# Spectral product by one inverse matmul: real and imaginary rows exchanged by DMA

## The chip, the cores and the metric

The kernel runs on one core of a Trainium2 chip. The metric is device time in microseconds, the median of several runs; one further execution was profiled. The engines are named as in the profile: PE (TensorE matmul; PEld is its weight load), DVE (VectorE), ACT (ScalarE), POOL (GpSimd) and SP (SyncE, which issues most DMAs).

## The reference, cut to what matters

Two layers follow each other. The first is an attention without softmax; the second is a long convolution by FFT between two gates. B is 8, S is 3136, D is 256, and z has 64 columns.

```python
scores = z @ z.T / S
x = u * (np.maximum(scores, 0) ** 2 @ v)          # 8 x 3136 x 256

x1, x2, x3 = split(x @ w_proj, 3)                 # 3136 x 256 each
X2 = rfft(x2, axis=1); H = rfft(filter_fft, axis=0)
y = x1 * irfft(X2 * H, axis=1) * x3
out = y @ w_out
```

`X2 * H` is a product of complex numbers, for each frequency and column. It is what the change is about.

## The kernel before, in words

**Attention.** A batch has 25 tiles of 128 rows (`NT`) and is worked through in seven chunks of 384 to 512 columns (`CHUNKS`). For each pair of tiles PE makes scores (L1238), ACT applies relu into `R_t` (L1388), DVE or ACT squares into `A_t` (L1397, L1395), and PE weighs the rows of v with the squares (L1266). The scores are symmetric, so squares of up to two chunks ahead are not computed again: SP issues DMA transposes of `A_t` into mirror tiles (`M_t`, `M2e_t`, `M2o_t`, L1351). An `A_t` buffer (there are 8) is free when its weighing and its transposes are done.

**Projection.** DVE multiplies the sum by u into `xT_t` (L1437). Then PE makes x1 and x3 (L821, L833), whose product goes to a tile of the ring `gate` (L839; 22 tiles, two a chunk), and x2 (L867).

**Convolution.** The transform of length 3136 is done as 64 x 49. A first stage (L699) works on x2 and stores its result to a scratch in DRAM (L706). When a batch is complete, `add_spectrum` runs over its 32 values of q in eight groups of four. For each group, SP loads four slices (L729) and PE makes the forward transform with the table `S2` (L912), one matmul of 98x256 for each q. The 98 rows of the result are 49 frequencies with a real and an imaginary row each, side by side. Two evictions (`copy`, L337 on ACT or L341 on DVE) bring them to `xs_t`. Then DVE multiplies the group by the filter's real and imaginary parts into the two halves of `zs_t`, in one instruction of 98x2048 (L934). The filter table `H` holds both parts with each repeated on both rows of a frequency. PE makes the inverse transform with two matmuls for each q (L956): the table `TZ[0]` for the half with the real part, and `TZ[1]`, whose rows are exchanged and signed, for the half with the imaginary part. They add up in PSUM, so the exchange of real and imaginary rows that a complex product needs is done by the second table. Evictions to `gs_t` and a store (L979) follow. The inverse matmuls of a group are handed to the planner after the forward part of the next group.

**End.** `add_end` loads the result (L740), makes the last transform stage (L1010), multiplies by the gates into `yT_t` (L1017), multiplies by w_out (L1048), evicts to `ost_t` and stores (L1075).

**Order of the work.** A planner in the kernel's own Python writes the order of every engine's instructions. Each piece of work is a task with a cost, its dependencies, the buffers that it takes, and a priority. PE's tasks lie in queues: S for scores, W for weighing, FA for projection, FB for the spectrum and the end, FZ for what is held back to the last batch. Side work is mixed into W by a credit (`PACE` 0.6 us for each W task). The other engines take the task that can start first, and at equal times the lower priority number. A DMA's landing is planned as the end of its issue, plus `DMA_GO` of 1.2, plus its `moves` on one shared bus, plus `DMA_DONE` of 0.8, plus a `late` of its own. All engines then run their lists in order. The last batch (7) has nothing behind it; there the spectrum and the end use buffers of the attention as well, and the rest of batch 6's end fills the gaps.

**Start.** The tables are made on the chip in the first 160 us, while batch 0 already runs: `S2` by sines, `TZ` by transposes on PE (L641; L671 for the reversed one, out of tiles that DVE makes, L665 and L666), `H` by a transform of the filter (L781) with tables from L768.

Of the kernel before, what the change touches and what calls it, by code (L numbers as in the profile page):

```python
# [11 lines left out]
P = 128  # L12
# [7 lines left out]
N2 = 49  # L20
NQ = 32
# [4 lines left out]
LATE_PUT, LATE_LOAD, LATE_TURN, LATE_C, LATE_D2 = 3.0, 1.0, 1.5, 2.5, 1.0  # L26
REACH = 2
# [211 lines left out]
def kernel(  # L239
# [59 lines left out]
    g_p = Pool("gate", 22, [P, 512], BF16)  # L299
# [3 lines left out]
    xs_p = Pool("xs", 2, [P, 4, D], BF16)  # L303
    zs_p = Pool("zs", 2, [P, 4, 2, D], BF16)
# [210 lines left out]
    TZ = const.tile([P, 2, NQ, KR], BF16, name="TZ")  # L515
    H = const.tile([P, NQ, 2, D], BF16, name="H")
# [117 lines left out]
    for q0 in range(0, NQ, 8):  # L634
        deps = [s2_done[q0], s2_done[q0 + 4]]
        box = {}

        def turn(q0=q0, box=box):
            box["p"] = bank(BF16)
            for i in range(8):  # L640
                nc.tensor.transpose(box["p"][:KR, ds(i * KR, KR)], S2[:KR, q0 + i, :], ident[:KR, :KR])  # L641

        def back(e, q0=q0, box=box):
            src = box["p"][:KR, 0 : 8 * KR].rearrange("p (q k) -> p q k", q=8)
            copy(e, TZ[:KR, 0, ds(q0, 8), :], src)

        tt = pe("FB", turn, c_pe(*[P] * 8), deps, takes=[ps_m.slots])
        tb = job(None, back, {"DVE": c_dve2(8 * KR)}, [tt], prio=3)
        tb.frees.append((tt, 0))
        tz_done.append(tb)  # L650
        if q0 == 0:
            tz_done.append(
                on(
                    "DVE",
                    lambda: nc.vector.tensor_single_scalar(TZ[0:2, 0, 0, :], TZ[0:2, 0, 0, :], 0.5, ALU.mult),
                    0.25, [tb],
                )
            )
        jbox = {}

        def sj(q0=q0, jbox=jbox):
            t = l_p.tile([P, 8, N2, 2], BF16)
            jbox["s"] = t
            sv = S2[:KR, ds(q0, 8), :].rearrange("p q (k c) -> p q k c", c=2)
            nc.vector.tensor_copy(t[:KR, :, :, 0], sv[:, :, :, 1])  # L665
            nc.vector.tensor_single_scalar(t[:KR, :, :, 1], sv[:, :, :, 0], -1.0, ALU.mult)  # L666

        def turnj(jbox=jbox):
            jbox["p"] = bank(BF16)
            for i in range(8):  # L670
                nc.tensor.transpose(  # L671
                    jbox["p"][:KR, ds(i * KR, KR)], jbox["s"][:KR, i, :, :].rearrange("p k c -> p (k c)"),
                    ident[:KR, :KR],
                )

        def backj(e, q0=q0, jbox=jbox):
            src = jbox["p"][:KR, 0 : 8 * KR].rearrange("p (q k) -> p q k", q=8)
            copy(e, TZ[:KR, 1, ds(q0, 8), :], src)

        ts = on("DVE", sj, 0.8, deps, [l_p.slots], prio=3)  # L680
        tt = pe("FB", turnj, c_pe(*[P] * 8), [ts], takes=[ps_m.slots])
        tt.frees.append((ts, 0))
        tb = job(None, backj, {"DVE": c_dve2(8 * KR)}, [tt], prio=3)
        tb.frees.append((tt, 0))
        tz_done.append(tb)
# [72 lines left out]
    for qq in range(NQ // 4):  # L758
# [3 lines left out]
        def tabs(qq=qq, tbox=tbox):  # L762
            t = gs_p.tile([P, 4, 2, KR], BF16)
            tbox["t"] = t
            for i in range(2):
                o = t[:KR, :, i, :].rearrange("p q (k c) -> p q k c", c=2)
                s = S2[:KR, ds(qq * 4, 4), :].rearrange("p q (k c) -> p q k c", c=2)
                nc.vector.tensor_copy(o, s[:, :, :, i].unsqueeze(3).to_broadcast([KR, 4, N2, 2]))  # L768
            if qq == 0:
                nc.vector.tensor_copy(t[:KR, 0, 0, 1:2], S2[:KR, 0, 1:2])  # L770
                nc.vector.memset(t[:KR, 0, 1, 0:2], 0.0)

        tb = on("DVE", tabs, 0.8, [s2_done[qq * 4], ld], [gs_p.slots], prio=3)
        for i in range(4):
# [11 lines left out]
            def ev(e, q=q, box=box):  # L786
                copy(e, H[:KR, q, :, :].rearrange("p i d -> p (i d)"), box["p"][:KR, :], h_scale)

# [103 lines left out]
    def add_spectrum(b, puts):  # L892
        deps0 = list(h_done) + list(tz_done) if b == 0 else []
        lasts = []
        prev = None
        for qq in range(8):
            own = b < B - 1 or qq % 2 == 0
            xh, zh, gh = (xs_p, zs_p, gs_p) if own else (xT_p, R_p, A_p)
            ld, ibox = load_spec(D1[b % 2], qq, puts, LATE_LOAD * (b < B - 1))
# [3 lines left out]
            for h in range(2):  # L903
                box = {}

                def mm(qq=qq, h=h, box=box, xb=xb, ibox=ibox, xh=xh, zh=zh):
                    box["p"] = bank()
                    if h == 0:
                        xb["x"], xb["z"] = xh.tile([P, 4, D], BF16), zh.tile([P, 4, 2, D], BF16)
                    for i in range(2):  # L910
                        q = qq * 4 + h * 2 + i
                        nc.tensor.matmul(  # L912
                            box["p"][:KR, ds(i * D, D)], S2[:KR, q, :], ibox["t"][:KR, h * 2 + i, :],
                            start=True, stop=True,
                        )

                def ev(e, h=h, box=box, xb=xb):
                    copy(e, xb["x"][:KR, ds(h * 2, 2), :].rearrange("p q d -> p (q d)"), box["p"][:KR, :])

                a = pe(  # L920
                    "FB", mm, c_pe(D, D), [ld, *deps0, *firsts],
                    [ps_m.slots] + ([xh.slots, zh.slots] if h == 0 else []),
                )
# [8 lines left out]

            def mul(qq=qq, xb=xb):
                nc.vector.tensor_tensor(  # L934
                    xb["z"][:KR], xb["x"][:KR].unsqueeze(2).to_broadcast([KR, 4, 2, D]),
                    H[:KR, ds(qq * 4, 4), :, :], ALU.mult,
                )

            z_ = on("DVE", mul, c_dve2(8 * D), evs)
            z_.frees.append((a0, 1))  # L940

            def inv(qq=qq, xb=xb, z_=z_, a0=a0, gh=gh):
# [3 lines left out]
                for h in range(2):  # L946
                    box = {}

                    def mm(h=h, box=box):
# [3 lines left out]
                        for i in range(2):  # L953
                            q = qq * 4 + h * 2 + i
                            for k in range(2):
                                nc.tensor.matmul(  # L956
                                    box["p"][:KR, ds(i * D, D)], TZ[:KR, k, q, :], xb["z"][:KR, h * 2 + i, k, :],
                                    start=(k == 0), stop=(k == 1),
                                )

                    def ev(e, h=h, box=box):
# [3 lines left out]
                        "FB", mm, c_pe(D, D, D, D), [z_, *firsts],  # L965
# [3 lines left out]
                    if h == 0:  # L969
                        g0 = a  # L970
                    else:
                        a.frees.append((a0, 2))
# [8 lines left out]
                p_ = on("SP", put, 0.4, es, moves=1.0, late=LATE_D2 * (b < B - 1))  # L981
# [3 lines left out]
            if prev:  # L985
                prev()
            prev = inv
        prev()
# [4 lines left out]
    def add_end(b, lasts, gtasks, tg, kind="FB", src=l_p, dsts=(o_p,), late=0, behind=(), then=()):  # L993
        for t0, nt in tg:
# [7 lines left out]
            for dh in range(2):  # L1002
# [26 lines left out]
                e_ = on("DVE", ev, 0.068 * pieces + w * 0.00104, [a], prio=2 + late)  # L1029
# [95 lines left out]
    def casts_at(b, c):  # L1125
# [3 lines left out]
        if n < B and 0 <= i < 4:  # L1129
            t0, t1 = 8 * i, min(8 * i + 8, NT)  # L1130

            def go_z(tick_):
# [27 lines left out]
                z_tasks.setdefault(n, []).append(t)  # L1160

# [199 lines left out]
    for gi, g in enumerate(groups):  # L1361
# [16 lines left out]
        for i, un in enumerate(g):  # L1378
# [40 lines left out]
            if last:  # L1419
# [27 lines left out]
                if c == NC - 1:  # L1447
# [9 lines left out]
                    else:  # L1457
                        add_end(b, lasts, gts, ends, "FB", A_p, (R_p, zs_p))
# [53 lines left out]
```

## Time and profile before

| what | value |
|---|---|
| runs | 1083.94 us median of 3 (1081.19 to 1084.87) |
| profiled execution | 1083.45 us, span 1081.7 us, mean granted clock 0.988 |
| PE | 1029.6 us busy, 6517 recorded matmuls |
| ACT, DVE, POOL | 910.7, 811.2, 184.8 us busy |
| DMA | 324112 packets, 167.44 MB, mean 155 GB/s |
| L956, inverse matmuls in PSUM tile `ps_m_t` | 456 recorded, mean 275 ns |
| L934, product with the filter, 98x2048 | 60, mean 1219 ns |
| L979, stores of the inverse transform | 60 of 196 KB |

The page of the profile gives for each engine its busy time, its share of the span and its instructions. The span is then cut into 40 slices, with a digit of tenths for each. The chain is followed back from the last instruction to what released each step. Groups of instructions stand by line, engine and tile. Matmuls are pipelined: a record lasts longer than the step from one matmul's start to the next. A small share of the matmul records is missing.

### The profile page before, as it was taken

The numbers are of one execution on the slowest core, as the hardware profiler recorded it, in microseconds if no ns is written. First come the engines' busy times: TensorE is split into PE (matmuls) and PEld (weight loads), VectorE is DVE, ScalarE is ACT, GpSimd is POOL, SyncE is SP. The second block draws the span as 40 slices with busy tenths as digits, with TensorE's granted clock in tenths as the row PEclk, the third lists the DMA queues.
The fourth block names the chain that finished last, engine by engine and source line by source line (L and its number), as shares of the span: only waits on it lengthen the run. The fifth ranks groups of instructions, "written<-read, shape, count | busy, mean of one in ns | idle before, by whom it ended". The sixth has DMA issues, their size and how long they took to land.

```text
span 1081.7 us, 18827 instructions
## 1 busy us (share of the span) xinstructions
PE 1029.6 (95%) x6517; PEld 545.9 (50%) x6591; DVE 811.2 (75%) x1277; ACT 910.7 (84%) x1265; POOL 184.8 (17%) x351
## 2 busy tenths in 40 slices
PE   5999899999999999999999999999999999999974
PEld 2444545545455455555455554555555554555563
DVE  7976679778777686977877687876878668776673
ACT  6987799888888888987889898898979879798763
POOL 2022202121112210122021211121112220011000
PEclk9999999999999999999999999999999999999987
DMA  7488938886798978898688878898788996755556
GB/s 150 94 143 161 178 74 165 155 165 153 168 151 141 175 143 154 177 156 182 136 185 154 162 148 174 163 151 170 161 164 146 137 182 132 186 115 124 131 171 215
DMA packets 324112, 167.44 MB, mean 155 GB/s; under 512 B 231968, under 2 KB 293792, under 8 KB 324016
## 3 DMA queue, kind: packets, MB, share of 16 engines
q1 hardware_dynamic: 301552, 135.58, 57.1%
q0 software_dynamic: 22464, 30.65, 20.4%
q8 instruction: 52, 0.85, 0.3%
q14 instruction: 44, 0.36, 0.1%
HBM read 89.62 MB, written 53.05 MB: 132 GB/s over the span
## 4 chain that ended last, share of the span: by engine, by line
PE 84%; DVE 6%; DMA 5%; issue 2%; ACT 2%; POOL 0%; SPq 0%; DVEq 0%; ACTq 0%; POOLq 0%
PE ps_o_t L1266 44%; PE ps_s_t L1238 11%; PE ps_m_t L956 4%; PE ps_m_t L833 4%; PE ps_m_t L821 4%; PE ps_m_t L867 4%; PE ps_m_t L1048 4%; DMA M_t<-A_t 3%; PE ps_m_t L912 2%; PE ps_m_t L699 2%; DVE A_t L1397 2%; PE ps_m_t L1010 2%; DVE xT_t L1437 1%; ACT A_t L1395 1%; PE ps_m_t L781 1%
## 5 line engine op out<-in xcount | busy, mean ns | idle before, releaser
L1388 ACT ACTIVATE R_t<-ps_s_t 128x1024 f32<-128x1024 f32 (+3 forms) x552 | 484.2, 913 | 45.0 <-PE ps_s_t L1238 28.7
L1266 PE MATMUL ps_o_t<-A_t,v_t 128*128 128x512 bf16 (+2 forms) x2121 | 489.8, 355 | 5.6 <-issue 1.7
L1266 PEld LDWEIGHTS <-v_t 128*128 128x128 bf16 x2800 | 264.7, 98 | 210.7 <-issue 33.1
L1397 DVE TENSOR_TENSOR A_t<-R_t 128x1024 bf16<-128x1024 f32 (+3 forms) x298 | 320.8, 1085 | 53.9 <-ACT R_t L1388 22.1
L1395 ACT ACTIVATE A_t<-R_t 128x768 bf16<-128x768 f32 (+3 forms) x254 | 237.1, 940 | 25.2 <-DMA M_t<-A_t 10.8
L375 POOL COPY tick<-xT_t 1x1 bf16<-1x1 bf16 x54 | 42.5, 786 | 788.8 <-DVE xT_t L1437 759.0
L1238 PE MATMUL ps_s_t<-zT_t 64*128 64x512 bf16 (+2 forms) x1088 | 155.2, 359 | 1.9 <-DVE zT_t L341 0.8
L1437 DVE SCALAR_TENSOR_TENSOR xT_t<-ps_o_t,uT_t 128x384 bf16<-128x384 f32 (+2 forms) x128 | 69.9, 556 | 48.2 <-PE ps_o_t L1266 31.2
L341 DVE CAST x_t<-ps_m_t 128x512 bf16<-128x512 f32 (+3 forms) x121 | 72.7, 613 | 26.9 <-PE ps_m_t L867 18.1
L839 DVE TENSOR_TENSOR gate_t<-ps_m_t,x_t 128x512 bf16<-128x512 f32 (+2 forms) x112 | 67.3, 620 | 27.3 <-PE ps_m_t L833 21.5
L1238 PEld LDWEIGHTS <-zT_t 64*128 64x128 bf16 x1088 | 32.8, 94 | 101.1 <-issue 97.8
L934 DVE TENSOR_TENSOR zs_t<-xs_t,H 98x2048 bf16<-98x2048 bf16 x60 | 73.0, 1219 | 10.4 <-ACT xs_t L337 9.8
L1266 PE MATMUL ps_o_t<-M_t,v_t 128*128 128x384 bf16 (+2 forms) x336 | 79.4, 345 | 0.0
L956 PE MATMUL ps_m_t<-zs_t,TZ 98*98 98x256 bf16 x456 | 68.7, 275 | 4.1 <-ACT xs_t L337 3.5
L1017 DVE TENSOR_TENSOR yT_t<-ps_m_t,gate_t 128x128 bf16<-128x128 f32 (+3 forms) x163 | 62.7, 425 | 12.1 <-PE ps_m_t L1010 11.9
L956 PEld LDWEIGHTS <-TZ 98*98 98x98 bf16 x512 | 59.0, 126 | 24.2 <-issue 13.5
L337 ACT ACTIVATE x_t<-ps_m_t 128x512 bf16<-128x512 f32 (+3 forms) x106 | 55.8, 540 | 15.5 <-PE ps_m_t L821 13.1
L370 POOL DMA_DIRECT2D un_t<-in_u_dram x112 | 59.8, 553 | 6.9 <-issue 5.3
L821 PE MATMUL ps_m_t<-xT_t,wp 128*128 128x384 bf16 (+2 forms) x214 | 57.7, 353 | 2.1 <-DVE xT_t L1437 1.4
L867 PE MATMUL ps_m_t<-wp,xT_t 128*128 128x256 bf16 x392 | 59.4, 273 | 0.2
L337 ACT ACTIVATE gs_t<-ps_m_t 98x512 bf16<-98x512 f32 x80 | 47.4, 603 | 13.8 <-PE ps_m_t L956 13.6
L1048 PE MATMUL ps_m_t<-wo,yT_t 128*128 128x256 bf16 (+1 forms) x360 | 56.1, 276 | 0.9 <-DVE yT_t L1017 0.6
(157 smaller groups left out, 937.6 us busy)
## 6 DMA issues: line engine op xcount, KB each, us to landing
out_dram<-ost_t SPq DMA_DIRECT2D x82, 256.0 KB
spec_in_t<-spec SPq DMA_DIRECT2D x64, 196.0 KB
spec<-gs_t SPq DMA_DIRECT2D x60, 196.0 KB
spec<-s_t SPq DMA_DIRECT2D x80, 128.0 KB
spec_in_t<-spec SPq DMA_DIRECT2D x39, 256.0 KB
v_t<-in_v_dram POOLq DMA_DIRECT2D x72, 128.0 KB, 4.7
un_t<-in_u_dram POOLq DMA_DIRECT2D x56, 128.0 KB, 5.9
un_t<-in_u_dram POOLq DMA_DIRECT2D x56, 96.0 KB, 4.4
```

The costliest lines, as they stand in the source:

```text
L337: nc.scalar.activation(out_, in_, AF.Copy)
L821: nc.tensor.matmul(box["p"][:, :cw], wp16[:, k, ds(nb * P, P)], xt["t"][:, k, :cw], start=(k == 0), stop=(k == 1),)
L867: nc.tensor.matmul(box["p"][:rows, ds(k_ * D, D)], xt["t"][:, k, ds((i + k_) * P, rows)], wp16[:, k, ds(D, D)], start=(k == 0), stop=(k == 1),
L934: nc.vector.tensor_tensor(xb["z"][:KR], xb["x"][:KR].unsqueeze(2).to_broadcast([KR, 4, 2, D]), H[:KR, ds(qq * 4, 4), :, :], ALU.mult,)
L956: nc.tensor.matmul(box["p"][:KR, ds(i * D, D)], TZ[:KR, k, q, :], xb["z"][:KR, h * 2 + i, k, :], start=(k == 0), stop=(k == 1),)
L1048: nc.tensor.matmul(box["p"][:rows, ds(i * D, D)], yb["y"][:, k, ds((i0 + i) * P, rows)], wo16[:, k, :], start=(k == 0), stop=(k == 1),)
L1238: nc.tensor.matmul(ps[:m, i, :cw], zt[h, ds(t * P, m)], zt[h, ds(C0[c], cw)], start=True, stop=True)
L1266: nc.tensor.matmul(o, row(v16[b], t)[:, ds(dh * P, P)], x, start=(k == 0 and i == 0), stop=(last and i == len(pair) - 1),)
L1388: nc.scalar.activation(box["R"][:rows, 0:n, :cw], live[un][:rows, 0:n, :cw], AF.Relu)
L1395: nc.scalar.activation(a, r, AF.Square)
L1397: nc.vector.tensor_tensor(a, r, r, ALU.mult)
L1437: nc.vector.scalar_tensor_tensor(x, f, inv_s2, ut, ALU.mult, ALU.mult)
```

## The change

In batches 0 to 6 the exchange of real and imaginary rows moves ahead of the product. The forward transform is evicted into the first half of a tile `xh_t` (three buffers of two halves, in place of two `xs_t` and two `zs_t`). SP issues two DMAs from SBUF to SBUF, 49 rows each, which copy the even rows of the first half to the odd rows of the second, and the other way round. DVE multiplies both halves by the filter in one instruction of 98x2048, in place, and subtracts the second half from the first in another of 98x1024. PE then needs one inverse matmul for each q. The sign lies in the imaginary part of `H`, whose layout puts the two parts of a group of four q behind each other. The tables of the filter's transform (L768 before) take a third instruction for it.

In the last batch the two inverse matmuls stay. The product is two DVE instructions of 98x1024, and the reversed table is a copy of `TZ` with exchanged rows, made by two DMAs of 49 rows into a free `zT_t` tile once the last batch's z is transposed. The transposes on PE and the DVE work that made `TZ[1]` at the start go.

Beside it: the inverse part of a group follows two groups behind the forward part (`SPEC_LAG` 2; one in the last batch), the ring `gate` has 26 tiles for 22, and the product with the gates (L1017) has priority `late` for `2 + late`.

```diff
+LATE_SWAP, SPEC_LAG = 1.0, 2
-    g_p = Pool("gate", 22, [P, 512], BF16)
+    g_p = Pool("gate", 26, [P, 512], BF16)
-    xs_p = Pool("xs", 2, [P, 4, D], BF16)
-    zs_p = Pool("zs", 2, [P, 4, 2, D], BF16)
+    xh_p = Pool("xh", 3, [P, 2, 4, D], BF16)
-    TZ = const.tile([P, 2, NQ, KR], BF16, name="TZ")
-    H = const.tile([P, NQ, 2, D], BF16, name="H")
+    TZ = const.tile([P, NQ, KR], BF16, name="TZ")
+    H = const.tile([P, NQ // 4, 2, 4, D], BF16, name="H")
...
-        def sj(q0=q0, jbox=jbox):
-            t = l_p.tile([P, 8, N2, 2], BF16)
...
-        def turnj(jbox=jbox):
...
-        def backj(e, q0=q0, jbox=jbox):
...
+    def swap_tz():
+        tj.append(zT_p.tile())
+        src = TZ[:KR].rearrange("(k c) q n -> c k (q n)", c=2)
+        dst = tj[0][:KR, 0 : NQ * KR].rearrange("(k c) n -> c k n", c=2)
+        for c in range(2):
+            nc.sync.dma_start(out=dst[1 - c], in_=src[c])
+
+    def load_tj(deps):
+        tj_task.append(on("SP", swap_tz, 0.9, deps, [zT_p.slots], prio=1, moves=2.0))
...
-            for i in range(2):
-                o = t[:KR, :, i, :].rearrange("p q (k c) -> p q k c", c=2)
-                s = S2[:KR, ds(qq * 4, 4), :].rearrange("p q (k c) -> p q k c", c=2)
-                nc.vector.tensor_copy(o, s[:, :, :, i].unsqueeze(3).to_broadcast([KR, 4, N2, 2]))
+            o = t[:KR].rearrange("p q i (k c) -> p q i k c", c=2)
+            s = S2[:KR, ds(qq * 4, 4), :].rearrange("p q (k c) -> p q k c", c=2)
+            nc.vector.tensor_copy(o[:, :, 0], s[:, :, :, 0].unsqueeze(3).to_broadcast([KR, 4, N2, 2]))
+            nc.vector.tensor_copy(o[:, :, 1, :, 0], s[:, :, :, 1])
+            nc.vector.tensor_single_scalar(o[:, :, 1, :, 1], s[:, :, :, 1], -1.0, ALU.mult)
...
+            def swap(xb=xb):
+                v = xb["z"][:KR].rearrange("(k c) i q d -> c k i (q d)", c=2)
+                for c in range(2):
+                    nc.sync.dma_start(out=v[1 - c, :, 1], in_=v[c, :, 0])
+
             def mul(qq=qq, xb=xb):
-                nc.vector.tensor_tensor(
-                    xb["z"][:KR], xb["x"][:KR].unsqueeze(2).to_broadcast([KR, 4, 2, D]),
-                    H[:KR, ds(qq * 4, 4), :, :], ALU.mult,
-                )
-
-            z_ = on("DVE", mul, c_dve2(8 * D), evs)
...
+                nc.vector.tensor_tensor(xb["z"][:KR], xb["z"][:KR], H[:KR, qq], ALU.mult)
+                nc.vector.tensor_tensor(xb["x"][:KR], xb["z"][:KR, 0], xb["z"][:KR, 1], ALU.subtract)
+
+            def mul2(qq=qq, xb=xb):
+                for i in (1, 0):
+                    nc.vector.tensor_tensor(xb["z"][:KR, i], xb["x"][:KR], H[:KR, qq, i], ALU.mult)
+
+            if final:
+                z_ = on("DVE", mul2, 2 * c_dve2(4 * D), evs)
+            else:
+                w_ = on("SP", swap, 0.9, evs, moves=0.55, late=LATE_SWAP)
+                z_ = on("DVE", mul, c_dve2(8 * D) + c_dve2(4 * D), [w_])
...
+                            if not final:
+                                nc.tensor.matmul(
+                                    box["p"][:KR, ds(i * D, D)], TZ[:KR, q, :], xb["x"][:KR, h * 2 + i, :],
+                                    start=True, stop=True,
+                                )
+                                continue
                             for k in range(2):
+                                w = TZ[:KR, q, :] if k == 0 else tj[0][:KR, ds(q * KR, KR)]
                                 nc.tensor.matmul(
-                                    box["p"][:KR, ds(i * D, D)], TZ[:KR, k, q, :], xb["z"][:KR, h * 2 + i, k, :],
+                                    box["p"][:KR, ds(i * D, D)], w, xb["z"][:KR, k, h * 2 + i, :],
                                     start=(k == 0), stop=(k == 1),
                                 )
...
-            if prev:
-                prev()
-            prev = inv
-        prev()
+            behind.append(inv)
+            if qq >= (1 if final else SPEC_LAG):
+                behind.pop(0)()
+        for x in behind:
+            x()
...
-                e_ = on("DVE", ev, 0.068 * pieces + w * 0.00104, [a], prio=2 + late)
+                e_ = on("DVE", ev, 0.068 * pieces + w * 0.00104, [a], prio=late)
...
+                if n == B - 1 and t1 == NT:
+                    load_tj([t])
```

## The prediction

> **What bounds the kernel now.** I read the page's busy line and slices, then the chain that ended last, the waits, the stretches of 40 us, and the timeline around one inverse transform. Times are those of the profiled execution: 1083.45 us, a span of 1081.7 and 1.75 around it; the median of the runs, 1083.94, is half a microsecond away.
>
> ```profile
> PE 1029.6 (95%) x6517; PEld 545.9 (50%) x6591; DVE 811.2 (75%) x1277; ACT 910.7 (84%) x1265; POOL 184.8 (17%) x351
> ...
> DMA  7488938886798978898688878898788996755556
> ...
> q1 hardware_dynamic: 301552, 135.58, 57.1%
> q0 software_dynamic: 22464, 30.65, 20.4%
> ...
> PE 84%; DVE 6%; DMA 5%; issue 2%; ACT 2%; POOL 0%; SPq 0%; DVEq 0%; ACTq 0%; POOLq 0%
> ```
>
> PE is busy 95% and holds 84% of the chain. Beside it, ACT at 84% and 16 DMA engines at 78% (57.1 + 20.4) are not far below. The stretches say more (PE, PEld, DVE, ACT, POOL busy, then clock, DMA share, GB/s):
>
> ```profile
> 320.00:360.00 40.00, 37.81 (x228) 20.60 (x228) 28.09 (x37) 33.80 (x48) 9.06 (x14) 0.96 0.98 147
> ...
> 440.00:480.00 40.00, 39.75 (x255) 22.11 (x256) 34.47 (x44) 36.86 (x54) 9.38 (x15) 1.00 0.85 155
> ...
> 840.00:880.00 40.00, 37.95 (x239) 20.23 (x239) 25.41 (x34) 32.07 (x45) 9.91 (x20) 1.00 1.00 159
> ```
>
> Of the 21 stretches from 160 to 1000 us, 18 leave PE idle 0.34 us each in the mean; the three in which the DMA share is 0.92 or more (320, 800, 840) leave 2.05. So PE is the bound, except where the DMA engines are full; such a stretch costs 1.7 us more. The chain and the waits show how it reaches PE:
>
> ```profile
> 821.09 8.01 DMA M_t<-A_t
> ...
> 843.13 7.97 DMA M_t<-A_t
> ```
> ```profile
> ACT A_t L1395 <- DMA M_t<-A_t: 10.8, 6, 2.7
> ...
> DVE A_t L1397 <- DMA M_t<-A_t: 8.3, 5, 3.4
> ```
>
> A mirror transpose that lands after 8 us keeps a buffer of A, so a square waits, and then PE. The chain has five such pieces (8.19, 6.46, 6.49, 8.01, 7.97).
>
> **The change, part by part.**
>
> (1) *One inverse matmul in place of two, batches 0 to 6.* The built order of PE has 512 matmuls on L956 now and 224 + 64 after: 224 of 98x256 less. Their price comes from the timeline:
>
> ```profile
> 448.59 0.60 PE L956 MATMUL ps_m_t<-zs_t,TZ 98*98 98x256 bf16 x4
> 449.02 1.03 PE L1266 MATMUL ps_o_t<-A_t,v_t 128*128 128x512 bf16 x4
> ```
>
> The next matmul starts 0.43 us after the first of the four: 108 ns each, not the 272 ns of one record, since they are pipelined. 224 x 0.108 = 24.2 us off a PE that waits for little. The Trainium skill (Trainium Kernel Development and Optimization, Performance Expectations) warns that matmul busy time is a bad metric of closeness to roofline. The trace agrees as to the metric: the whole program's columns at 0.108 us per 256 make some 937 us (estimate), not 1029.6. By that page the gain could be nothing; but the groups in the timeline start back to back, so I keep 24.2.
>
> (2) *The difference on DVE.* The page has L934, 98x2048, at 1219 ns x60; it stays one instruction per group of four q. New is a subtraction of 98x1024; no row has it. It lies between nothing and 1219 ns; half the elements in the same form gives 0.64 us. 56 x 0.64 = 36 us. In the built order DVE gives 11 squares to ACT (298 to 287; 11 x 1.08 = 12 us, and 11 x 0.94 = 10 us on ACT). DVE comes to about 835 of some 1065 us (78%), ACT to 921 (86%). PE's stream covers it; without that cover, in the spectrum's stretch (440: ACT 36.86 and DVE 34.47 of 40), it would cost some 5 us a batch. I take 2 us in all, bounds 0 and 10; the built order has spread the spectrum over more W work, so the load there thins.
>
> (3) *The exchange by DMA.* 56 pairs of SBUF copies, 49 rows of 2 KB each: 5488 packets. In the trace's packets, sorted by size, one of 2048 B on q1 took 103 ns: 5488 x 0.103 = 565 us of engine time, 35 us of 16 engines, if spread evenly. SP issues 112 more, at 0.34 to 0.58 us (rows L729, L706): 1 us a pair, beside 631 us of issue in all (58% of the span). What is queued behind a swap that waits for its eviction: mirror transposes, spectrum loads and stores, all on SP. The product then waits for the landing with DVE's squares and evictions behind it. The planner leaves it 1.2 + 0.55 + 0.8 + 1.0 = 3.55 us after issue. A comparable store (L979, 98 rows of 2 KB) landed 2.13 us after the end of its issue, 2.78 at the 90th percentile, so that most swaps are in time. On PE the built order has 7 to 28 us of other streaming between a group's last forward and its first inverse matmul (2 to 12 before; SPEC_LAG does that), so PE does not wait for a swap itself. The cost is what fuller engines do to the transposes. Its bounds: nothing (the even spread, 83%), and every spectrum stage full: 7 stages x 60 us = 10.5 stretches x 1.7 = 18 us. I take 8, near the middle, since 440:480 with share 0.85 cost PE nothing.
>
> The spread decides. A 98-row store raised its semaphore 15 times, once at issue and 14 times from 1.75 to 2.2 us; 128-row ones raise it 16 times as they land. I read 14 engines with seven rows each; 49 rows would then use seven, and both copies of a pair the same seven. Each gets 14 x 0.103 = 1.44 us a pair, 81 us in all: 842 + 81 = 923 of 1065, 87%, and in a spectrum stage (60 us at 0.83, plus 8 x 1.44 = 11.5) 61 of 60. The Trainium skill (DMA: Bandwidth & Descriptors, Why a DMA increments its semaphore by 16 and not by 1) says so too: the number of engines is the largest up to 16 that divides the slowest dimension, 7 for 49. That rule speaks against this change; by it the sum would stand at the upper bound, 18 in place of 8.
>
> (4) *Start.* 32 transposes (L671, 2.1 us), DVE's reversed tables (L665, L666: 3.1 us) and four copies to TZ (4 x 0.56 us) go; the filter tables get a third, smaller instruction (8 x about 0.2). The start waits for other things as well (PE 36.6 of 40 in 80:120), so -1 us, bounds 0 and -4.
>
> (5) *Tail, ring, priority.* The last batch keeps two inverse matmuls and copies the reversed TZ once, 614 KB, long ahead. Two products of 98x1024 (0.64 each) replace 1.22: eight times 0.06. Five groups instead of four are in flight. Four more gates keep the next batch's projection from waiting while the spectrum runs later; yT, with a higher priority, frees a PSUM bank sooner. 0, bounds -4 and +4.
>
> Sum: 1083.45 - 24.2 + 2 + 8 - 1 + 0 = 1068.
>
> **Rivals.**
>
> *Engines full in every spectrum stage.* For: seven of 16 engines at 61 of 60 us. Against: 0.85 cost nothing, and the planner counts the bus. 18 in place of 8: 1078.
>
> *Slower: the mirror transposes hold A.* Place: L1395 and L1397 waiting for M_t<-A_t. For: five chain pieces of 6.5 to 8.2 us already, all where the share is high, and swaps are put between these transposes on SP and on the same engines. Price: PE's idle time in the stretches around them, about 1.9 us each. Point: 13 new ones (25 us), two a batch, eat the gain. With three in each of seven batches: 21 x 1.9 = 40, so 1083.45 - 24.2 + 40 = 1099. Against: the swaps last 11.5 us a batch on their engines, and most of a batch has none.
>
> *All of it hidden.* The swaps cost nothing, and the start and the reordering give their 4 us each: 1083.45 - 24.2 - 8, some 1052.
>
> *No change, since PE isn't the bound (the busy metric):* 1083; I count it with the second case's upper part.
>
> **How the numbers follow.** Forecast 0.52; full stages 0.18 (half of it faster, 0.07 within 0.3%, 0.02 slower); slower 0.16; all hidden 0.14. About 0.3% (3.3 us) is what a measurement can tell from no change. Faster 0.52 + 0.14 + 0.09 = 0.75, same 0.07, slower 0.18. The forecast's own range is 1058 to 1076; the range of 1050 to 1088 takes in the full stages and most of the hidden case, and leaves out the slower one's larger part.
>
> **What would show it.** In the changed profile: PE busy down by about 24 us with its idle time per stretch still near 0.4; one line of 224 inverse matmuls; a subtraction near 0.64 us x56; waits of DVE's product for a DMA that are short; semaphores of the swaps raised by seven engines; DMA share in spectrum stretches near 0.9. Wrong would be: M_t<-A_t waits on ACT and DVE well over 21 us, products waiting microseconds for the swap, or PE's idle time in most stretches near 2 us.

## The result, and the profile after

The changed kernel takes 1130.48 us (median of 4 runs, 1126.96 to 1137.35), the kernel before beside it 1084.4: a ratio of 1.0433 (1.0376 to 1.0491). It is 46 us slower where 1068 was forecast. Its profiled execution took 1130.62 us.

The page of the changed kernel, with the lines that answer to those shown of before, and with its own new rows:

```profile
span 1128.8 us, 18522 instructions
...
PE 1022.1 (91%) x6261; PEld 521.3 (46%) x6335; DVE 832.6 (74%) x1326; ACT 917.1 (81%) x1276; POOL 175.8 (16%) x351
...
DMA  7596737977799778998689777988679969885567
...
q1 hardware_dynamic: 307936, 147.43, 59.7%
q0 software_dynamic: 22464, 30.65, 19.5%
...
PE 62%; DMA 16%; DVE 8%; ACT 6%; issue 4%; SPq 3%; POOL 1%; DVEq 0%; ACTq 0%; POOLq 0%
...
L930 DVE TENSOR_TENSOR xh_t<-xh_t,H 98x2048 bf16<-98x2048 bf16 x56 | 68.4, 1222 | 45.5 <-DMA xh_t<-xh_t 44.1
...
xh_t<-xh_t SPq DMA_DIRECT2D x112, 98.0 KB
```

PE's busy time is lower (1022.1 for 1029.6 us), but in a longer span. Its part of the chain that ended last fell from 84% to 62%, and DMA's rose from 5% to 16%. The mean DMA share, 59.7 + 19.5 = 79%, is hardly above the 78% of before: from this line alone one would not suspect the DMAs. The L930 row points at them: of DVE's 45.5 us of idle time in front of the product, 44.1 ended with the landing of a swap.

The waits of the changed kernel (who waits <- for what: us in all, times, longest):

```profile
DVE xh_t L930 <- DMA xh_t<-xh_t: 44.1, 24, 4.3
...
DVE A_t L1410 <- DMA M_t<-A_t: 16.2, 7, 3.5
...
PE ps_o_t L1279 <- DMA M_t<-A_t: 9.3, 2, 8.5
DVE A_t L1410 <- DMA M2e_t<-A_t: 8.5, 1, 8.5
...
PE ps_m_t L959 <- DVE s_t L341: 7.7, 3, 3.1
ACT A_t L1408 <- DMA M2e_t<-A_t: 4.7, 2, 4.2
...
ACT A_t L1408 <- DMA M_t<-A_t: 3.3, 3, 2.9
```

The first line is new: 24 of the 56 products wait, up to 4.3 us each. The squares' waits for mirror transposes are 16.2 + 8.5 + 4.7 + 3.3 = 32.7 us. Before they were 10.8 + 8.3 + 2.3 = 21.4, with this line for the last term:

```profile
DVE A_t L1397 <- DMA M2e_t<-A_t: 2.3, 1, 2.3
```

How a wait of DVE reaches PE is seen in the stretch round 500 us. The swap was issued on SP, then DVE and PE (start, us, instruction, idle time before it and what ended it):

```profile
498.38 1.54 SPq L927 DMA_DIRECT2D xh_t<-xh_t  x2
```
```profile
501.95 1.22 DVE L1410 TENSOR_TENSOR A_t<-R_t 128x1024 bf16<-128x1024 f32 x1
505.22 1.23 DVE L930 TENSOR_TENSOR xh_t<-xh_t,H 98x2048 bf16<-98x2048 bf16 x1 [2.06 <-DMA xh_t<-xh_t]
506.48 0.69 DVE L931 TENSOR_TENSOR xh_t<-xh_t 98x1024 bf16<-98x1024 bf16 x1
507.09 0.69 DVE L341 CAST s_t<-ps_m_t 128x512 bf16<-128x512 f32 x1
```
```profile
507.83 0.38 PE L959 MATMUL ps_m_t<-xh_t,TZ 98*98 98x256 bf16 x2 [1.73 <-DVE s_t L341]
```

The product is at the head of DVE's list from about 503.2 to 505.22, while the swap is under way. Behind it stands the eviction of `s_t`, which has nothing to do with the spectrum. PE needs the bank that this eviction frees, and is idle for 1.73 us. No row of PE names the swap: PE waits for DVE, and DVE for the DMA.

The same in stretches of 40 us (PE, PEld, DVE, ACT, POOL, clock, DMA share, GB/s):

```profile
480.00:520.00 40.00, 34.84 (x197) 17.33 (x198) 29.48 (x38) 28.78 (x41) 7.18 (x17) 0.96 0.87 160
520.00:560.00 40.00, 39.84 (x265) 20.69 (x267) 29.14 (x52) 34.66 (x47) 5.98 (x14) 1.00 0.75 151
...
720.00:760.00 40.00, 31.49 (x169) 14.69 (x168) 24.95 (x33) 24.05 (x34) 8.12 (x14) 0.87 0.94 154
```

In a spectrum stretch (480, 720) all engines have idle time at once; between two spectra (520) PE is as full as before. Over the 21 stretches from 160 to 1000 us PE is idle 2.66 us each in the mean. Counted by the relus done (the same work in both kernels), the changed kernel is 2.8 us ahead at the 46th, 5.2 behind at the 69th (a batch has about 69), 14.4 at the 115th, 25.4 at the 253rd, 36.5 at the 391st, 48.2 at the 551st. So the loss is a stall near the start of about 8 us, some 9 up to the 115th, where the first spectrum lies, and then 5 to 6 in every batch.

### The profile page after: what moved, and what is told of

The parts are those of the page before. It is cut to its first block, busy times and chain, and to the rows that moved or that the text cites. A ratio compares the mean times of both kernels' runs of the same rounds, so it can differ in the third digit from the quotient of the medians.

```text
span 1128.8 us, 18522 instructions
## 1 busy us (share of the span) xinstructions
PE 1022.1 (91%) x6261; PEld 521.3 (46%) x6335; DVE 832.6 (74%) x1326; ACT 917.1 (81%) x1276; POOL 175.8 (16%) x351
## 3 DMA queue, kind: packets, MB, share of 16 engines
q1 hardware_dynamic: 307936, 147.43, 59.7%
q0 software_dynamic: 22464, 30.65, 19.5%
## 4 chain that ended last, share of the span: by engine, by line
PE 62%; DMA 16%; DVE 8%; ACT 6%; issue 4%; SPq 3%; POOL 1%; DVEq 0%; ACTq 0%; POOLq 0%
PE ps_o_t L1279 33%; PE ps_s_t L1251 9%; DMA xh_t<-xh_t 7%; DMA M_t<-A_t 3%; PE ps_m_t L1059 3%; PE ps_m_t L855 3%; PE ps_m_t L809 3%; PE ps_m_t L821 3%; ACT R_t L1401 2%; DVE xh_t L930 2%; PE ps_m_t L686 2%; DMA M2e_t<-A_t 2%; PE ps_m_t L905 2%; PE ps_m_t L1021 2%; PE ps_m_t L959 2%
## 5 line engine op out<-in xcount | busy, mean ns | idle before, releaser
L1410 DVE TENSOR_TENSOR A_t<-R_t 128x1024 bf16<-128x1024 f32 (+3 forms) x287 | 308.0, 1081 | 58.2 <-ACT R_t L1401 27.7
L1408 ACT ACTIVATE A_t<-R_t 128x1024 bf16<-128x1024 f32 (+3 forms) x265 | 248.8, 947 | 18.4 <-PE ps_o_t L1279 7.8
L375 POOL COPY tick<-xT_t 1x1 bf16<-1x1 bf16 x54 | 32.5, 603 | 843.3 <-DVE xT_t L1450 792.7
L930 DVE TENSOR_TENSOR xh_t<-xh_t,H 98x2048 bf16<-98x2048 bf16 x56 | 68.4, 1222 | 45.5 <-DMA xh_t<-xh_t 44.1
L337 ACT ACTIVATE x_t<-ps_m_t 128x512 bf16<-128x512 f32 (+3 forms) x123 | 64.2, 544 | 25.1 <-PE ps_m_t L855 18.7
L1450 DVE SCALAR_TENSOR_TENSOR xT_t<-ps_o_t,uT_t 128x384 bf16<-128x384 f32 (+2 forms) x128 | 69.6, 557 | 19.5 <-PE ps_o_t L1279 13.7
L341 DVE CAST x_t<-ps_m_t 128x512 bf16<-128x512 f32 (+3 forms) x106 | 63.0, 610 | 25.5 <-PE ps_m_t L855 15.2
L855 PEld LDWEIGHTS <-xT_t 128*128 128x128 bf16 x400 | 37.8, 99 | 49.3 <-issue 34.0
L959 PE MATMUL ps_m_t<-xh_t,TZ 98*98 98x256 bf16 x224 | 42.6, 284 | 19.7 <-DVE s_t L341 7.7
L337 ACT ACTIVATE s_t<-ps_m_t 128x512 bf16<-128x512 f32 (+2 forms) x71 | 39.3, 560 | 22.4 <-PE ps_m_t L686 22.0
L809 PE MATMUL ps_m_t<-xT_t,wp 128*128 128x384 bf16 (+2 forms) x212 | 53.8, 352 | 0.7
L821 PE MATMUL ps_m_t<-xT_t,wp 128*128 128x384 bf16 (+2 forms) x213 | 54.1, 352 | 0.4
```

Source lines behind the costliest of these rows:

```text
L337: nc.scalar.activation(out_, in_, AF.Copy)
L809: nc.tensor.matmul(box["p"][:, :cw], wp16[:, k, ds(nb * P, P)], xt["t"][:, k, :cw], start=(k == 0), stop=(k == 1),)
L821: nc.tensor.matmul(box["p3"][:, :cw], wp16[:, k, ds((4 + nb) * P, P)], xt["t"][:, k, :cw], start=(k == 0), stop=(k == 1),)
L855: nc.tensor.matmul(box["p"][:rows, ds(k_ * D, D)], xt["t"][:, k, ds((i + k_) * P, rows)], wp16[:, k, ds(D, D)], start=(k == 0), stop=(k == 1),
L930: nc.vector.tensor_tensor(xb["z"][:KR], xb["z"][:KR], H[:KR, qq], ALU.mult)
L1408: nc.scalar.activation(a, r, AF.Square)
```

## The experiments

Theory: the swap's way (SP's list, seven engines, landing) costs more than one inverse matmul saves, above all since DVE's product waits for it in order. Rivals: the swaps' bytes crowd out the mirror transposes (the prediction's slower case); the reordered work and the start, apart from the swaps; the subtraction on DVE. All ratios are to the kernel before, run on the same chip.

### e1: the product planned later

```diff
-LATE_SWAP, SPEC_LAG = 1.0, 2
+LATE_SWAP, SPEC_LAG = 5.0, 2
```

> The changed kernel with the planner's extra for the landing of a swap (LATE_SWAP) at 5.0 us in place of 1.0, nothing else. Theory 1, late landings: the pair of copies lands 4.23 us (median) but 7.75 us (90th percentile) after its first issue, the plan allows 4.45, and 24 of 56 products wait 44 us in all at the head of DVE's list; with 8.45 us allowed those waits fall under 8 us in all and the time comes to 1085 to 1105. Theory 2, load: the copies make the DMA engines and SP too full, whatever is planned: still 1120 to 1140. Theory 3, the rest of the plan (start, ring, priority) is what costs: 1115 to 1135.

1117.01 us (1113.34 to 1135.55), 1.0283 (1.0253 to 1.0313). Four more microseconds of planned distance bring back 13, not all. The time lies above the range of theory 1 and below that of theory 2, in that of theory 3 alone, which e2 then speaks against. The profiled execution is the longest one, 1135.55 us, so its waits are not read. It stays open whether the rest is waiting or the copies' mere presence.

### e2: no exchange at all

```diff
-                nc.vector.tensor_tensor(xb["z"][:KR], xb["z"][:KR], H[:KR, qq], ALU.mult)
+                nc.vector.tensor_tensor(
+                    xb["z"][:KR], xb["x"][:KR].unsqueeze(1).to_broadcast([KR, 2, 4, D]), H[:KR, qq], ALU.mult
+                )
...
-                w_ = on("SP", swap, 0.9, evs, moves=0.55, late=LATE_SWAP)
```

> The changed kernel without the copies: the product reads the first half for both parts, so the exchange of real and imaginary rows is left out; the difference, the single inverse matmul, SPEC_LAG 2 and the priority stay (ring of 25 gates, two tiles for the product of their own). Theories 1 and 2: all that the copies cost is gone, 1060 to 1080. Theory 3: the 24 us of PE are had, but start and plan still cost, 1090 to 1110.

1072.17 us (1070.94 to 1073.41), 0.9886 (0.9863 to 0.9909): 58 us under the changed kernel. Without the copies the rest of the change is a gain of 12. So theory 3 falls. Two of e2's spectrum stretches:

```profile
320.00:360.00 40.00, 39.27 (x238) 19.93 (x239) 34.92 (x48) 39.54 (x57) 8.19 (x14) 1.00 0.88 157
560.00:600.00 40.00, 38.75 (x232) 19.91 (x234) 35.78 (x50) 39.19 (x56) 9.92 (x17) 1.00 0.83 155
```

PE is nearly full again, but so is ACT in these two (39.54 and 39.19 of 40), with DVE at 35. I read that the difference on DVE has pushed squares to ACT and that the cover is used up there; e12 tests it.

### e12: nor the difference

```diff
-                nc.vector.tensor_tensor(xb["x"][:KR], xb["z"][:KR, 0], xb["z"][:KR, 1], ALU.subtract)
```

(on top of e2; the inverse matmul reads `xb["x"]` as it is)

> The kernel without copies, and without the subtraction too (the product's two halves are made and the inverse matmuls read the first half as it was evicted; exchange and difference are left out). It has 39 us less on DVE (56 x 0.692). If the fuller ACT and DVE take the rest of PE's 24 us (11 of them came back without the copies): 1058 to 1066. If the difference is hidden, as the prediction had it: 1069 to 1075.

1062.09 us (1061.28 to 1064.06), 0.9806 (0.9777 to 0.9836). So PE's saving with all that goes beside it (`SPEC_LAG`, the ring, the priority, the start) is worth 1084 - 1062 = 22 us, and the difference on DVE, with the order that the planner makes for it, costs 1072 - 1062 = 10. PE's busy time is 1004.8 us, 24.8 less than before.

### e3, e5: the copies' load, but nobody waits

```diff
+                w_ = on("SP", swap, 0.9, evs, [dump_p.slots], moves=0.55, late=LATE_SWAP)
...
+                v = H[:KR, qq, 0].rearrange("(k c) q d -> c k (q d)", c=2)
+                o = dump_p.tile()[:KR].rearrange("(k c) q d -> c k (q d)", c=2)
+                for c in range(2):
+                    nc.sync.dma_start(out=o[1 - c], in_=v[c])
...
```

(on top of e2; e3 with one spare tile, e5 with two)

> As the kernel without the copies, but with the same 112 copies of 49 rows issued by SP, after the same evictions, from a constant table to a spare tile that nobody reads; so their load is there and no product waits for them (the exchange is left out). Theory 1: within 15 us of the kernel without copies, far below the changed one. Theory 2: within 15 us of the changed kernel (1115 or more).

> The kernel with unread copies once more, with two spare tiles in place of one (and 23 gates), since with one tile SP waited 42 us for the copies before it. If that wait made the 32 us over the kernel without copies: 1072 to 1085. If the copies' issue and bytes make it: 1095 to 1110. (The exchange is left out.)

e3: 1104.31 us, 1.0182 (1.0142 to 1.0222), between the ranges of both theories. With one spare tile SP itself waits for the copy before, as its queue's waits show:

```profile
SPq L929 <- DMA dump_t<-H: 41.9, 22, 4.7
```

So e3 mixes the load with a wait that the changed kernel doesn't have. e5 is without it: 1102.31 us (1101.92 to 1102.94), 1.0164 (1.012 to 1.0207), so that this wait was worth little. The copies cost 30 us over e2 though nothing reads them (with 23 gates for 25, and another order). The chain of e5 has DMA at 12%:

```profile
PE 65%; DMA 12%; ACT 9%; DVE 6%; issue 4%; SPq 2%; POOL 1%; ACTq 0%; DVEq 0%; POOLq 0%
```

### e6: the same issues, hardly a byte

```diff
-                v = H[:KR, qq, 0].rearrange("(k c) q d -> c k (q d)", c=2)
+                v = H[:KR, qq, 0, 0, 0:16].rearrange("(k c) n -> c k n", c=2)
```

(on top of e5; the spare tiles shrink to such rows; the same order of all instructions, rows of 32 B for 2048)

> The same instructions in the same order on every engine as with two spare tiles, but each unread copy has 32 bytes a row in place of 2048: SP's issue and its wait for the evictions stay, the bytes on the engines go. If SP's list is what costs: within 8 us of the run with full rows. If the seven engines are: near the kernel without copies, 1070 to 1080. (The exchange is left out.)

1082.5 us (1079.35 to 1085.11), 0.9977 (0.9956 to 0.9998). That is in neither range: both parts cost. Of e5's 30 us, 20 are the copies' bytes (e5 over e6, the same order on every engine). The other 10 (e6 over e2) go to the 112 instructions on SP, the two gates fewer and the other order together: in e6 eight instructions have moved from DVE to ACT. That the issues are the main part of the 10 is argued, not shown. The queue line of e6, where after has 307936, 147.43:

```profile
q1 hardware_dynamic: 307936, 136.37, 58.5%
```

As many packets, 11 MB less. One issue takes SP 0.737 us at 32 B a row and 0.740 at 2048, both medians: the issue's price does not hang on the bytes.

### e9: unread copies on 14 engines

```diff
-                for c in range(2):
-                    nc.sync.dma_start(out=o[1 - c], in_=v[c])
+                o = dump_p.tile()
+                for c in range(2):
+                    nc.sync.dma_start(out=o[:KR, ds(2 * c, 2), :], in_=H[:KR, qq, 0, ds(2 * c, 2), :])
```

(on top of e5; two copies of 98 rows of 1 KB, the same bytes and order)

> The unread copies (two spare tiles) as two of 98 rows of 1 KB in place of two of 49 rows of 2 KB: the same bytes, the same number of DMAs in the same order, on 14 engines in place of seven. (The exchange is left out.) If the seven engines make the 20 us between full and tiny rows: 1082 to 1090. If the bytes do, wherever they land: 1097 to 1107.

1096.42 us (1092.88 to 1104.95), 1.013 (1.0087 to 1.0172). That lies between the two ranges, and the interval overlaps that of e5: how much of the 20 us of bytes goes to seven engines rather than 14 is not settled by this pair; the medians differ by 6.

### e10: the real copies on 16 engines

```diff
-                v = xb["z"][:KR].rearrange("(k c) i q d -> c k i (q d)", c=2)
+                v = xb["z"][:].rearrange("(k c) i q d -> c k i (q d)", c=2)
```

(64 rows for 49, in three kept tiles whose rows 98 to 127 are zero; the order is that of the changed kernel, only the last stores use another pool's tiles)

> The changed kernel with the real copies over 64 rows in place of 49 (rows 98 to 127 hold zeros), so that they land on 16 engines with four rows each, the instructions in the same order; only the last stores use other buffers. If the seven engines make the landing late: a pair lands within 4 us in the median and 6 at the 90th percentile, products wait under 25 us, and the time is 1095 to 1112. If not: 1122 to 1138.

1097.73 us (1097.16 to 1103.85), 1.0129 (1.01 to 1.0157): 33 us under the changed kernel, with 31% more rows copied. The queue line counts a packet for each row, and more. Before has 301552, e2 301664, after 307936, and e10:

```profile
q1 hardware_dynamic: 310624, 150.88, 61.5%
```

e2 differs from after by the 112 copies: (307936 - 301664) / 112 = 56 packets each, 49 rows and 7 more. For e10 it is 80, 64 rows and 16 more. The semaphore updates in the traces give the same: a copy of 49 rows raises it 8 times, once at issue and seven times as it lands, and its seven further packets are of 4 B each; I read one raise from each of seven engines. A copy of 64 rows raises it 16 times. The waits in e10:

```profile
DVE xh L942 <- DMA xh<-xh: 18.2, 12, 3.0
DVE A_t L1422 <- DMA M_t<-A_t: 14.1, 7, 5.7
...
DVE A_t L1422 <- DMA M2e_t<-A_t: 7.3, 1, 7.3
ACT A_t L1420 <- DMA M_t<-A_t: 5.0, 4, 2.4
...
ACT A_t L1420 <- DMA M2e_t<-A_t: 2.4, 1, 2.4
```

Twelve products wait 18.2 us in place of 24 for 44.1, and a pair of copies lies 3.35 us (median; 6.50 at the 90th percentile) from first issue to last landing, for 4.23 and 7.75. All came as expected but the 90th percentile, where 6 was the limit. A copy's issue took 0.58 us, for 0.73: e10 changes the spread and SP's list, 64.5 us of issues for 82.6, and does not separate them.

### e4: an even spread bought with more DMAs

```diff
-                    nc.sync.dma_start(out=v[1 - c, :, 1], in_=v[c, :, 0])
+                    nc.sync.dma_start(out=v[1 - c, lo:hi, 1], in_=v[c, lo:hi, 0])
```

(for `lo, hi` in 0:48 and 48:49, so four DMAs a group)

> The changed kernel with each copy cut in 48 rows and 1 row, so that 48 rows land on 16 engines (three rows each) in place of seven with seven rows; SP issues four DMAs a group in place of two, 0.73 us each. If the seven engines are what makes landings late: the pair lands sooner after its last issue, waits of the product under 30 us, the time under 1120. If issue and the queue ahead of the copies matter: the landing after the first issue gets later by 1 us or more, waits over 44 us, 1130 to 1160.

1150.91 us, 1.0614 (1.0584 to 1.0644), the slowest of all. 224 issues of 0.58 us (median) are 134 us of SP in place of 82.6, and the product waits longer than in any other kernel:

```profile
DVE xh_t L931 <- DMA xh_t<-xh_t: 66.4, 28, 6.1
...
DVE A_t L1411 <- DMA M_t<-A_t: 7.3, 6, 2.9
DVE A_t L1411 <- DMA M2e_t<-A_t: 5.5, 2, 3.1
...
ACT A_t L1409 <- DMA M_t<-A_t: 0.5, 1, 0.5
```

Its packets on SP's queue are 96 for each 49 rows, as (312416 - 301664) / 112. I read 48 rows and 16, and the last row in 16 pieces and 16: an even spread. Wait and time came as expected for issue and queue; the landing did not. Counted from the first issue the four copies land as the pair did (4.32 us in the median and 7.65 at the 90th percentile, for 4.23 and 7.75), and after the last issue sooner (1.77 us in the median, for 2.69). DVE, ACT and POOL have the same order as in the changed kernel. So a spread alone doesn't help if SP's list grows for it.

### e11: the copies issued by POOL

```diff
-                w_ = on("SP", swap, 0.9, evs, moves=0.55, late=LATE_SWAP)
+                w_ = on("POOL", swap, 1.1, evs, moves=0.55, late=LATE_SWAP)
...
-                    nc.sync.dma_start(out=v[1 - c, :, 1], in_=v[c, :, 0])
+                    nc.gpsimd.dma_start(out=v[1 - c, :, 1], in_=v[c, :, 0])
```

(`LATE_SWAP` 3.0)

> The changed kernel with the copies issued by POOL in place of SP, LATE_SWAP 3.0. If SP's list is the larger part: SP's issue time falls by 83 us and the time to 1085 to 1110, unless POOL's own list, which waits for the steps of the attention, lands them later: then products wait over 44 us and the time is 1130 or more.

1091.95 us (1084.12 to 1098.23, 10 runs), 1.0066 (1.0036 to 1.0095): 39 under the changed kernel, with the same bytes read and waited for. Its profiled execution is one of its shortest, 1085.48 us. No product waits for a swap in it, although the copies land no sooner: 4.54 us from the first issue in the median, 7.33 at the 90th percentile. The plan allows 2 us more after the issue. POOL, idle for four fifths of the span, takes the issues at 0.53 us each; SP is back at 657 us of issue from 747 (before 631). The copies' packets are 48 each on POOL's queue and not 56, and 24 of them are of 4096 B, two rows; so their rows are cut otherwise too: e11 changes the issuer, the planned distance and possibly the spread.

### e7, e13: the start as it was

```diff
+        jbox = {}
+
+        def sj(q0=q0, jbox=jbox):
...
+        tb = job(None, backj, {"DVE": c_dve2(8 * KR)}, [tt], prio=3)
```

(the work of the reversed table put back at the start, written to a tile that nobody reads; e7 on e2, e13 on e11)

In the changed kernel the start has a stall. SP's waits for the loads of u, its list there, then PE:

```profile
SPq L1116 <- DMA un_t<-in_u_dram: 22.8, 4, 7.4
```
```profile
125.30 1.30 SPq L1116 DMA_TRANSPOSE uT_t<-un_t  x1
126.69 0.54 SPq L693 DMA_DIRECT2D specf<-s_t  x1
127.28 1.36 SPq L1364 DMA_TRANSPOSE M_t<-A_t  x1
```
```profile
134.20 1.65 PE L1279 MATMUL ps_o_t<-M_t,v_t 128*128 128x448 bf16 x4 [8.49 <-DMA M_t<-A_t]
```

A transpose of `un_t`, whose load came late, holds the mirror transpose behind it on SP, and PE waits 8.49 us for that, 5.6 of them after the issue's end.

> The kernel without copies, with the start's work of before put back (the reversed tables' DVE work, 32 transposes and copies, into a tile that nobody reads; the exchange is left out). Theory: the changed start only moved its order so that a load of u came late, SP waited 7 us for it and PE 8.5 us for a mirror transpose behind it; with the old start work these are gone and the time is 1062 to 1067. Rival: the start is not it, 1070 to 1076.

> The changed kernel with the copies issued by POOL (LATE_SWAP 3.0) and the start's work of before put back. Theory: the start's stall (some 8 us lost by the last of batch 0's scores) is a term of its own: 1080 to 1086, below the 1092 with POOL alone. Rival: what is lost at the start is given back later, as without copies, where putting it back gave nothing: 1088 to 1096.

e7: 1075 us (1070.63 to 1078.61), 0.9918 (0.9887 to 0.9948). The stall was gone, and the time is not better than e2's: here my theory of the start fell. e13: 1072.47 us (1071.77 to 1079.24), 0.9896 (0.9862 to 0.9929): 19 us better than e11 by the same edit, and below both ranges of its expectation. Why it is worth nothing without copies and 19 with POOL's is open; an order that shifts everything behind it is one guess, and no run tests it. e13 does the whole computation and beats both kernels. With the start as it was, the exchange issued by POOL takes no more than no exchange at all (e7, 1075); with the changed start it costs 20 us (e11 over e2). No run puts the start back with the copies on SP.

### e8: a priority alone

```diff
-                e_ = on("DVE", ev, 0.068 * pieces + w * 0.00104, [a], prio=2 + late)
+                e_ = on("DVE", ev, 0.068 * pieces + w * 0.00104, [a], prio=late)
```

(the kernel before, with only the priority of the product with the gates changed)

> The kernel before with only the priority of the product with the gates changed (late for 2 + late). If the priority is a part of the loss: 1090 or more. If not: 1080 to 1088; a gain below 1080 would say that it helps.

1079.94 us (1078.49 to 1083.3), 0.9968 (0.9948 to 0.9988): at most a small gain, and no part of the loss.

## Why the prediction was wrong

The step that failed is (3), the exchange by DMA: it was priced at 8 us and cost 58. The medians as a ladder. Only e6 and e5 have the same order of instructions; at the other steps the planner's order changes too, and the ring of gates at some, so that these steps are rough:

| kernel | us | step |
|---|---|---|
| before | 1084 | |
| e12: one inverse matmul and what goes beside it, no difference, no copies | 1062 | -22 |
| e2: and the difference on DVE | 1072 | +10 |
| e6: and 112 issues on SP | 1082 | +10 |
| e5: and their bytes, on seven engines | 1102 | +20 |
| after: copies that the product waits for | 1130 | +28 |

Three kernels with the real copies have the same order on DVE, ACT and POOL, but for e10's zeros and last stores. Theirs is the cleaner comparison (us; the waits are those of the lines above):

| kernel | SP's issues of the copies | products' wait for them | squares' wait for mirror transposes | time |
|---|---|---|---|---|
| e10 | 64.5 | 18.2 | 28.8 | 1098 |
| after | 82.6 | 44.1 | 32.7 | 1130 |
| e4 | 134.0 | 66.4 | 13.3 | 1151 |

The time follows the products' wait and SP's issues, and not the squares' wait. e4 and e10 are both spread over 16 engines, by the raises of their semaphores, and stand at the two ends, so SP's list counts beside the spread. How the 33 us between e10 and the changed kernel divide between the two is open.

A part of the loss may be PE's clock. The granted clock is lower in some of the stretches in which PE has idle time (0.96 and 0.87 in the rows 480 and 720 above); over the span it is 0.973, for 0.985 in e2. That makes (1 - 0.973) x 1128.8 - (1 - 0.985) x 1071.6 = 14 us of clock, an estimate, and an upper bound for its part of the 58 us between the two. That the clock fell because PE stood idle is a guess that no run tests.

**(1) PE's saving** was right: 24.2 forecast, 22 found with what goes beside it, and PE's busy time in e12 fell by 24.8. The prediction's 937 us for the columns of the whole program is wrong: the recorded matmuls of before stream 2.44 million columns, which at 0.108 us per 256 make 1030 us, as much as PE's busy time. The Trainium skill (Trainium Kernel Development and Optimization, Performance Expectations) warns that matmul busy time is a bad metric of closeness to roofline. As a measure of this saving it did well in e12; in the changed kernel it fell by only 7.5 us while the profiled time rose by 47, a part of which may be the lower clock.

**(2) The difference on DVE** was mis-sized, 2 for 10, the upper bound. The instruction itself came close, 692 ns for 640 (half of 1219 would have been 610). The rows of 2048 and 1024 elements, 1222 and 692 ns, differ by 530; so the smaller one pays 162 ns beside its elements. The Trainium skill (VectorE: DVE Perf Modes, The TRN2 errata — SBUF-src ops pay a fixed extra latency per instruction) measures some 150 cycles at 0.96 GHz for such a fixed term. At that clock the 530 ns are half a cycle an element; with the 151 cycles that the Trainium skill has in the same section, there for fp32, the estimate is (512 + 151) / 0.96 = 691 ns, and the trace agrees. What failed is "the load there thins": the two stretches of e2 above leave ACT less than one microsecond of 40, so the cover was thinner than in the stretch of before that I went by (ACT 36.86).

**(3) The exchange by DMA** failed. It had 8 us, with bounds 0 and 18; against e2 it costs 58. Three things were mis-sized or missing.
- *"so that most swaps are in time"*. The planner's distance from the first issue is 4.45 us; a pair took 4.23 (median), 7.75 (90th percentile), 8.42 at most. So 32 of 56 were in time and 24 were not; 24 products wait, most of them for these. The model for it, a store that lands 2.13 to 2.78 us after its issue, gave the median well (2.43) and the tail not at all (5.87 at the 90th percentile); the second issue of a pair adds to it (1.52 us for both, 1 assumed). And the step named DVE's squares and evictions behind the waiting product, but priced only what fuller engines do to the transposes. The wait with what stands behind it was the largest term, some 28 us by the difference to e5. Two kernels with different orders stand behind this figure, so it is rough; but e10, with 26 us less of such waits in the same order, is 33 better, and e4, with 22 more, 20 worse.
- *SP's list*. The "1 us a pair" was set beside 631 us of issue in all and then not charged. Issues of 32 B rows came with 10 us (e6 over e2, with what else differs there), and e4's 51 us more of issues with 20.
- *The bytes on seven engines*. The reading of the semaphore was right, and the upper bound of 18 (each stretch full, at 1.7 us) lies near the 20 that e5 costs over e6; whether by the mechanism that the bound stands for, full stretches, no run shows. The Trainium skill (DMA: Bandwidth & Descriptors, Why a DMA increments its semaphore by 16 and not by 1) says that the number of engines is the largest up to 16 that divides the slowest dimension; the trace agrees (8 raises of the semaphore, 49 + 7 packets, 64 + 16 in e10). I gave that case a chance of 0.18, though it rested on a row and a rule that agreed.

**(4) The start** was given -1. Its order changed and brought a stall of about 8 us instead; what it is worth in the end is open (0 in e7, 19 in e13). **(5)** was not tested by itself apart from the priority (e8).

**The slower rival** had the right sign and the wrong place. Its waits did grow, 21.4 to 32.7 us, with 9.3 of PE behind the start's stall; but in e2, without copies, PE's 9.2 us stand as well, and the time is good, and in e4, the slowest, the squares' waits are 13.3. The main place was the product at the head of DVE's list, which the prediction named among what would show it wrong ("products waiting microseconds for the swap") and gave no rival of its own.

## What to carry to other kernels

A DMA put between two instructions of an engine that works in order is to be priced by the tail of its landing under this kernel's load, with everything that stands behind the waiting instruction, and not by its median alone. The issue is a cost too, on the list of whoever issues: with the changed start the same exchange cost 58 us from SP and 20 from POOL with 2 us more of planned distance (after and e11 over e2). A mean DMA share says little of a copy that runs on seven engines; count its rows, its packets, or the raises of its semaphore.

## What the runs showed of the hardware

- The issue of a copy from SBUF to SBUF went by its shape and its engine here, not by its bytes: 0.74 us for 49 rows of 32 or of 2048 B, 0.81 for 98 rows of 1 KB, 0.58 for 64 rows of 2 KB (medians of e6, e5, e9, e10, from SP; e9's and e5's reach 1.7 and 1.4), 0.53 from POOL (e11).
- An issue can be held up. In the changed kernel a mirror transpose, 1.24 us in the median, took 6.36 on SP in the first spectrum (SP's timeline). The longest of the kernel before took 3.48, and of e13, with its swaps issued by POOL, 5.97, so that what holds it is open:

```profile
197.16 6.36 SPq L1364 DMA_TRANSPOSE M_t<-A_t  x1
```

- More rows can be faster: a pair of copies lands 3.35 us after its first issue with 64 rows (16 raises of the semaphore) and 4.23 with 49 rows (8 raises), and even the issue is shorter (0.58 us for 0.73).
- Two issuers cut the same copy otherwise: 49 rows of 2 KB are 49 packets of a row each from SP (the changed kernel), and 24 of two rows and one of 2052 B from POOL (e11), beside packets of 4 and 8 B.
